# Gated linear attention with experts: scores of two heads beside each other, by halves of the keys

## Chip, core, metric

One Trainium2 chip, of which the kernel uses one core. The time is that of the device for one execution, in microseconds, as the median of several. The engines named below are TensorE (PE; its weight loads are listed apart as PEld), VectorE (DVE), ScalarE (ACT), GpSimd (POOL) and SyncE (SP, which only issues DMAs here).

## What is computed

A linear attention whose state decays by a complex factor at each step, then a top-1 mixture of 8 experts on its rows (B=4, H=8, S=768, D=48; 3072 tokens, 384 features, expert width 1024). Cut to what matters:

```python
for t in range(S):
    ar, ai = a_re_n[:, :, t, :, None], a_im_n[:, :, t, :, None]   # |a| at most 0.999
    S_re, S_im = ar * S_re - ai * S_im + k_t v_t^T, ar * S_im + ai * S_re
    y[:, :, t] = q_t @ S_re
x = y as (B*S, H*D)
e_idx = argmax(x @ w_gate);  gate_w = softmax(...)[e_idx];  eom = sigmoid(x @ w_output_gate)
out[mask] = gate_w * eom * (relu(x[mask] @ w1[e]) @ w2[e])       # mask: e_idx == e
```

Within a tile of 128 time steps the output of query `t` needs the keys `s <= t` of the tile alone and the state before the tile. So a tile costs a matrix of scores (keys by queries, masked to `s <= t`), its product with `v`, and a product of the queries with the state.

## The kernel before

The tokens are cut into 24 tiles of 128 steps (6 tiles for each of 4 batches), and the attention stage goes through them in order; the experts' stage follows it. All matmuls that matter here are f32.

For tile `i` the functions inside `attention` do this:

- `decay`, `turns`, `phase` (a side chain that runs ahead of the tiles): cumulative sums of log-magnitude and phase by matmuls with triangles (L510, L563), a carry of the phase from one tile to the next (L565, or a small DMA of one row, L573), and cosine and sine on ACT into `trig`. The last row of the decay goes through a DMA `rcs` (L519) and a transpose into `rc`.
- `turn`: on DVE, `k` and `q` times cosine and sine (`kc`, `qc`: 128 x 8 heads x 96, L611); on PE eight transposes each into PSUM, on ACT two copies into `kt` and `qt` (96 rows, 8 heads x 128 columns, L621).
- `score` (twice, four heads each): per head one matmul, stationary `kt` of the head (96 rows, 128 columns), moving `qt` (128 columns), into 128 columns of a PSUM bank `sc` (L653); then on DVE one product with a mask into `scores` (L654).
- `state`: the state that the tile leaves, through matmuls with 32 stationary columns (L638), the former state being added by a matmul with the identity (L633).
- `values`: per pair of heads (`j`, `u` = 0 or 1), stationary `v` of the head (48 columns) and moving `scores` (L667), then stationary state and moving `qt` (L673), both into PSUM partitions 0 to 47 for `u` = 0 and 64 to 111 for `u` = 1 of the same tile `xo`; ACT copies it to `xt` (L677).
- `finish` and `gates`: four transposes of `xt`, rows out to `xd` (L700), logits by matmuls with 32 stationary columns (L233).

An f32 matmul stands in the trace as two records, a transpose as one.

PE, DVE and ACT keep an order that is laid out when the kernel is built: the functions are generators, `main` takes the tiles' steps, `step_aside` the side chain's, and the pace and the priorities (`urge`) decide how they are interleaved. Loads are issued on SP's queue in the order of the program; `loads` hands them out as tiles are done: `k`, `q`, `v` have seven buffers each (`AHEAD`), so the load of tile `i + 7` waits for the last reader of tile `i`.

## Time and profile before

| | us |
|---|---|
| median of 3 runs (lowest, highest) | 530.51 (528.88, 531.61) |
| the profiled execution | 532.94 |
| its span, first to last instruction | 531.1 |
| mean granted TensorE clock | 0.975 of full speed |
| PE busy with scores, L653 (384 records) | 51.2 |
| PE busy with values, L667 (384 records) | 41.4 |
| DVE busy with the masked copies, L654 (48) | 32.6 |

The attention stage ends, and the experts' stage begins, at about 283 us. "Busy" is the time in which an engine had at least one instruction in work; PE's records overlap each other, so the busy time of a group is more than its share of the stream. In rows by group, the columns are line, engine, operation, tiles as out<-in, shapes and count, busy us and mean ns of one, and idle time ahead with what ended it. In rows of the timeline they are start, time, engine, line, operation, tiles, shape (stationary rows*columns, then the moving operand), and count.

### The profile page before, as it was taken

What the parts mean: (1) busy time and instruction counts of PE and PEld (TensorE: products, weight loads), DVE (VectorE), ACT (ScalarE), POOL (GpSimd) and SP (SyncE); (2) the same over time, 40 slices, a digit from 0 to 9 for tenths busy, and PEclk for the clock granted to TensorE, in tenths of its full rate; (3) what the DMA queues carried; (4) which work ended last, traced back from release to release, by engine and by line L of the source; (5) the groups of instructions that cost most, each with busy time, mean ns of one, the idle gap of its engine ahead of it and who ended that gap; (6) DMA issues with size and microseconds to landing.
All of it is one profiled execution on the core that took longest, in us unless ns stands there. A gap on an engine that the chain in (4) does not pass through costs nothing.

```text
span 531.1 us, 11170 instructions
## 1 busy us (share of the span) xinstructions
PE 493.5 (93%) x4297; PEld 420.3 (79%) x4297; DVE 337.3 (64%) x775; ACT 319.0 (60%) x603; POOL 121.1 (23%) x131
## 2 busy tenths in 40 slices
PE   2799897998999999999899999999999999999992
PEld 0376565776777778878678889999999999999992
DVE  4578869895998899987685646355453726345220
ACT  7689678985879888767533447355453727354220
POOL 4000201030040503051350554412333222011112
PEclk9799989998999999999999999999999999999997
DMA  8664452534334321014560576525263644330001
GB/s 274 199 231 150 74 165 69 161 77 114 124 76 136 58 90 41 29 31 136 138 207 0 149 191 198 153 101 206 47 209 114 200 123 147 139 135 30 21 22 45
DMA packets 47523, 63.86 MB, mean 120 GB/s; under 512 B 12383, under 2 KB 39290, under 8 KB 47460
## 3 DMA queue, kind: packets, MB, share of 16 engines
q1 hardware_dynamic: 39332, 53.64, 33.8%
q0 software_dynamic: 8128, 9.42, 6.1%
q8 instruction: 36, 0.59, 0.5%
q14 instruction: 27, 0.22, 0.2%
HBM read 53.92 MB, written 9.88 MB: 120 GB/s over the span
## 4 chain that ended last, share of the span: by engine, by line
PE 57%; issue 17%; DMA 7%; DVE 7%; POOL 4%; ACT 4%; SPq 1%; POOLq 0%; DVEq 0%; ACTq 0%
PE up L1225 13%; PE acc L1163 12%; PE tr L95 8%; PE sc L653 4%; PE cs L563 4%; PE xo L667 3%; POOL out_dram L1176 3%; PE cs L510 3%; DMA carry<-ai 2%; PE xo L673 2%; PE st L638 2%; DMA ar<-in_a_re_dram 2%; PE cs L565 1%; POOL rows L1104 1%; PE xt L95 1%
## 5 line engine op out<-in xcount | busy, mean ns | idle before, releaser
L1230 DVE SCALAR_TENSOR_TENSOR hl<-up,hh 128x464 fp32r<-128x464 f32 (+7 forms) x64 | 37.7, 589 | 68.8 <-ACT hh L1229 67.5
L1229 ACT ACTIVATE hh<-up 128x464 fp32r<-128x464 f32 (+7 forms) x64 | 33.1, 518 | 74.0 <-PE up L1225 72.7
L1225 PE MATMUL up<-xh,w1h 128*128 128x464 f32 (+7 forms) x192 | 68.6, 357 | 0.0
L1225 PE MATMUL up<-xl,w1h 128*128 128x464 f32 (+7 forms) x192 | 67.6, 352 | 0.0
L1225 PE MATMUL up<-xh,w1l 128*128 128x464 f32 (+7 forms) x192 | 67.5, 351 | 0.0
L1163 PE MATMUL acc<-hh,w2h 128*128 128x464 f32 (+6 forms) x168 | 61.4, 366 | 0.0
L1176 POOL DMA_INDIRECT out_dram<-y,sid x28 | 31.8, 1135 | 124.5 <-ACT y L1198 121.6
L1163 PE MATMUL acc<-hl,w2h 128*128 128x464 f32 (+6 forms) x168 | 59.4, 356 | 0.0
L1163 PE MATMUL acc<-hh,w2l 128*128 128x464 f32 (+6 forms) x168 | 59.3, 353 | 0.0
L653 PE MATMUL sc<-qt,kt 96*128 96x128 f32 x384 | 51.2, 277 | 0.0
L653 PEld LDWEIGHTS sc<-qt,kt 96*128 96x128 f32 x384 | 47.3, 192 | 2.4 <-issue 1.1
L1104 POOL DMA_INDIRECT rows<-xd,sid x28 | 37.3, 1333 | 51.4 <-DVE w1l L203 22.6
L1059 POOL DMA_INDIRECT table<-entry,addr x20 | 31.4, 1571 | 65.3 <-DVE addr L1055 59.0
L203 DVE TENSOR_TENSOR w1l<-raw,w1h 128x512 fp32r<-128x512 f32 x48 | 30.5, 686 | 20.4 <-ACT w1h L202 17.3
L667 PE MATMUL xo<-scores,v 128*48 128x128 f32 x384 | 41.4, 279 | 0.0
L202 ACT CAST w1h<-raw 128x512 fp32r<-128x512 f32 x48 | 26.9, 619 | 17.0 <-DMA raw<-in_moe_w_dram 17.0
L1225 PEld LDWEIGHTS up<-xl,w1h 128*128 128x128 f32 x192 | 36.0, 188 | 1.2 <-DVE xl L1137 0.3
L1225 PEld LDWEIGHTS up<-xh,w1l 128*128 128x128 f32 x192 | 36.1, 188 | 1.0
L1225 PEld LDWEIGHTS up<-xh,w1h 128*128 128x128 f32 x192 | 36.1, 188 | 0.9
L203 DVE TENSOR_TENSOR w2l<-raw,w2h 128x512 fp32r<-128x512 f32 x48 | 30.5, 686 | 9.8 <-ACT w2h L202 7.4
L533 POOL COPY rcs<-rcs 24x48 f32<-24x48 f32 (+2 forms) x10 | 5.8, 579 | 134.0 <-DMA rcs<-re 86.9
L654 DVE TENSOR_TENSOR scores<-sc,mask 128x512 f32<-128x512 f32 x48 | 32.6, 681 | 5.0 <-PE sc L653 4.5
(214 smaller groups left out, 1125.2 us busy)
## 6 DMA issues: line engine op xcount, KB each, us to landing
raw<-in_moe_w_dram SPq DMA_DIRECT2D x32, 768.0 KB
ar<-in_a_re_dram SPq DMA_DIRECT2D x24, 192.0 KB
ai<-in_a_im_dram SPq DMA_DIRECT2D x24, 192.0 KB
k<-in_k_dram SPq DMA_DIRECT2D x24, 192.0 KB
q<-in_q_dram SPq DMA_DIRECT2D x24, 192.0 KB
v<-in_v_dram SPq DMA_DIRECT2D x24, 192.0 KB
xd<-xn SPq DMA_DIRECT2D x24, 192.0 KB
rows<-xd,sid POOLq DMA_INDIRECT x28
```

The source lines that it names most:

```text
L95: return nc.tensor.transpose(out=out, in_=in_, identity=ident[p0:p0 + n, p0:p0 + n])
L203: ins = nc.vector.tensor_tensor(out=lo[:, s], in0=raw[:, s], in1=hi[:, s].bitcast(F32), op=ALU.subtract)
L653: nc.tensor.matmul(sp[:, j * P:(j + 1) * P], r["kt"][:D2, h, :], r["qt"][:D2, h, :], start=True, stop=True)
L654: nc.vector.tensor_tensor(out=r["s"][:, 4 * hh:4 * hh + 4, :], in0=sp.rearrange("p (h t) -> p h t", t=P), in1=mask.unsqueeze(1).broadcast_ ...
L667: nc.tensor.matmul(op[u * DP:u * DP + D, j * P:(j + 1) * P], vt[c][:, h * D:(h + 1) * D], r["s"][:, h, :], start=True, stop=(cc == 0))
L1059: ins = nc.gpsimd.indirect_dma_start(out=table, out_offset=bass.IndirectOffsetOnAxis(ap=addr[:, c:c + 1], axis=0), in_=entry[:, c, :], in_ ...
L1104: nc.gpsimd.indirect_dma_start(out=rows[e % 2][:n, i, :], out_offset=None, in_=xd[:known], in_offset=bass.IndirectOffsetOnAxis(ap=ids[:n, ...
L1163: nc.tensor.matmul(accs[kt][:, :cap], w[:, cs], a, start=(ft == 0 and s == 0), stop=(ft == FT - 1 and s == 2))
L1176: ins = nc.gpsimd.indirect_dma_start(out=out, out_offset=bass.IndirectOffsetOnAxis(ap=ids(e)[:n, i:i + 1], axis=0), in_=y[:n, :], in_offse ...
L1225: nc.tensor.matmul(up[:, :cap], w[:, kt, :], x[:, kt, :], start=(m == 0), stop=(m == 3 * KT - 1))
L1229: nc.scalar.activation(out=hh, in_=up[:, :cap], func=AF.Relu)
L1230: nc.vector.scalar_tensor_tensor(out=hl, in0=up[:, :cap], scalar=0.0, in1=hh.bitcast(F32), op0=ALU.max, op1=ALU.subtract)
```

## The change

A matrix of scores has keys (rows) by queries (columns), and the block of later keys by earlier queries is zero. The change splits keys and queries into halves of 64. For two heads, the even one and the odd one of a pair, it makes three 64 x 64 blocks each, in four matmuls with 64 stationary columns instead of two with 128: the even head's first keys by all queries go to PSUM partitions 0 to 63, the odd head's first keys by all queries to partitions 64 to 127; the odd head's second keys by second queries to partitions 0 to 63, the even head's to 64 to 127. A pair then fills 3 x 64 columns over 128 partitions in place of 2 x 128, and the masked product reads 384 columns for four heads in place of 512.

In `values`, the first 64 queries of both heads share one block of 64 columns: its stationary operand is `vz`, a copy of `v` with zeros in the 64 rows of the other head. For the second 64 queries the even head's keys stand in order (stationary `v`) and the odd head's with halves exchanged (stationary `vs`). So each head gets two matmuls with 64 moving columns in place of one with 128. `vz` and `vs` are loaded by four more DMAs a tile (64 partitions, 192 elements, 48 KB each) into four buffers each; the zeros are written once by POOL. On the host, `v` is laid out with the even heads ahead of the odd ones; `at_v` is a head's place in it. POOL also makes the new `masks`.

```diff
+    at_v = lambda h: h % 2 * HP + h // 2
+    HALF = P // 2
...
+    masks = const.tile([P, 3, HALF], F32, name="masks")
+    nc.gpsimd.memset(masks, 1.0)
+    for p0, blocks in ((0, (0, 2)), (HALF, (0, 1))):
+        for n in blocks:
+            nc.gpsimd.affine_select(
...
+            VBUFS = 4
...
+            first_v = [pre.tile([P, H, D], F32, name=f"vz{n}") for n in range(VBUFS)]
+            for t in first_v:
+                nc.gpsimd.memset(t[HALF:, 0:HP, :], 0.0)
+                nc.gpsimd.memset(t[:HALF, HP:H, :], 0.0)
+            other_v = [pre.tile([P, HP, D], F32, name=f"vs{n}") for n in range(VBUFS)]
...
+            def loads_halves(i):
+                rows = v.rearrange("b (c x t) h d -> (b c) x t h d", x=2, t=HALF)[i]
+                z, o = first_v[i % VBUFS], other_v[i % VBUFS]
+                nc.sync.dma_start(out=z[:HALF, 0:HP, :], in_=rows[0, :, 0:HP, :])
+                nc.sync.dma_start(out=z[HALF:, HP:H, :], in_=rows[0, :, HP:H, :])
+                nc.sync.dma_start(out=o[:HALF], in_=rows[1, :, HP:H, :])
+                nc.sync.dma_start(out=o[HALF:], in_=rows[0, :, HP:H, :])
...
             def score(i, hh):
...
-                for j in range(4):
-                    h = 4 * hh + j
-                    nc.tensor.matmul(sp[:, j * P:(j + 1) * P], r["kt"][:D2, h, :], r["qt"][:D2, h, :], start=True, stop=True)
+                for j in range(2):
+                    e, o = 4 * hh + 2 * j, 4 * hh + 2 * j + 1
+                    kt, qt = r["kt"][:D2], r["qt"][:D2]
+                    to = sp[:, j * 3 * HALF:(j + 1) * 3 * HALF].rearrange("p (x t) -> p x t", t=HALF)
+                    parts = qt.rearrange("p h (x t) -> p h x t", t=HALF)
+                    nc.tensor.matmul(to[:HALF, 0:2, :], kt[:, e, :HALF], parts[:, e], start=True, stop=True)
+                    nc.tensor.matmul(to[HALF:, 0:3:2, :], kt[:, o, :HALF], parts[:, o], start=True, stop=True)
+                    nc.tensor.matmul(to[:HALF, 2, :], kt[:, o, HALF:], qt[:, o, HALF:], start=True, stop=True)
+                    nc.tensor.matmul(to[HALF:, 1, :], kt[:, e, HALF:], qt[:, e, HALF:], start=True, stop=True)
...
             def values(i):
...
+                vz, vs = first_v[i % VBUFS], other_v[i % VBUFS]
                 for j in range(HP):
+                    by_block = r["s"][:, j, :].rearrange("p (x t) -> p x t", t=HALF)
                     for u in range(2):
-                        h = 2 * j + u
                         nc.tensor.matmul(
-                            op[u * DP:u * DP + D, j * P:(j + 1) * P], vt[c][:, h * D:(h + 1) * D], r["s"][:, h, :],
-                            start=True, stop=(cc == 0))
+                            op[u * DP:u * DP + D, j * P:j * P + HALF], vz[:, at_v(2 * j + u), :], by_block[:, 0, :],
+                            start=True, stop=(cc == 0), skip_group_check=True)
+                    for u in range(2):
+                        nc.tensor.matmul(
+                            op[u * DP:u * DP + D, j * P + HALF:(j + 1) * P], vs[:, j, :] if u else vt[c][:, j * D:(j + 1) * D],
+                            by_block[:, 1 + u, :], start=False, stop=(cc == 0), skip_group_check=True)
...
             def loads():
+                while halves and st["done"] > halves[0] - VBUFS:
+                    loads_halves(halves.pop(0))
...
             loads_b(0, "v")
             loads_b(1, "v")
+            for i in range(2):
+                loads_halves(i)
             loads_b(2)
```

The rows below are the order in which instructions stand on an engine (line, operation, out<-in, shape of what is written, count). On PE, at the scores of tile 0, between the transposes of tile 1's `k` and `q`, before:

```order
L95 MATMUL tr<-ident,kc_162 96x128 x8
L653 MATMUL sc<-qt_165,kt_166 128x128 x4
L95 MATMUL tr<-ident,qc_161 96x128 x8
L653 MATMUL sc<-qt_165,kt_166 128x128 x4
L95 MATMUL cs<-ident,rcs 96x8
```

and after the change, up to the transposes of `q`:

```order
L97 MATMUL tr<-ident,kc_168 96x128 x8
L684 MATMUL sc<-qt_187,kt_188 64x128
L685 MATMUL sc<-qt_187,kt_188 64x2x64
L686 MATMUL sc<-qt_187,kt_188 64x64
L687 MATMUL sc<-qt_187,kt_188 64x64
L684 MATMUL sc<-qt_187,kt_188 64x128
L685 MATMUL sc<-qt_187,kt_188 64x2x64
L686 MATMUL sc<-qt_187,kt_188 64x64
L687 MATMUL sc<-qt_187,kt_188 64x64
L97 MATMUL tr<-ident,qc_167 96x128 x8
```

The place is the same; four matmuls that write 128 partitions have become eight that write 64, between neighbours that write 96. Later in the program the scheduler also puts other work inside a pair, as here, on PE at the scores of tile 2:

```order
L684 MATMUL sc<-qt_187,kt_188 64x128
L97 MATMUL tr<-ident,kc_168 96x128 x4
L97 MATMUL st<-ident,ls 128x128
L97 MATMUL tr<-ident,kc_168 96x128 x4
L685 MATMUL sc<-qt_187,kt_188 64x2x64
```

One matmul of the pair stands ahead of nine transposes, its partner behind them. On SP, the queue around the eighth `carry`, before:

```order
L519 DMA rcs<-re 8x1x48
L700 DMA xd<-xn 128x384
L365 DMA v<-in_v_dram 128x384
L573 DMA carry<-ai 1x16x24
L365 DMA k<-in_k_dram 128x384
```

and after:

```order
L547 DMA rcs<-re 8x1x48
L740 DMA xd<-xn 128x384
L410 DMA vz_173<-in_v_dram 64x192
L411 DMA vz_173<-in_v_dram 64x192
L412 DMA vs_185<-in_v_dram 64x192
L413 DMA vs_185<-in_v_dram 64x192
L601 DMA carry<-ai 1x16x24
L385 DMA v<-in_v_dram 128x384
L385 DMA k<-in_k_dram 128x384
```

The four loads of halves stand ahead of `carry`, and `v` behind it.

More of the change, by code (lines that the diff above doesn't have):

```diff
@@ L112, in tile_gated_attention_moe @@
     nc.gpsimd.tensor_copy(out=tri_o, in_=mask)
+    masks = const.tile([P, 3, HALF], F32, name="masks")
[3 more added lines that the diff above has]
+            nc.gpsimd.affine_select(
+                out=masks[p0:p0 + HALF, n, :], in_=masks[p0:p0 + HALF, n, :], pattern=[[1, HALF]], compare_op=ALU.is_ge,
+                fill=0.0, base=0, channel_multiplier=-1)
     tri_s = tri("tri_s", 1.0, strict=True, dt=BF16)
@@ L445, in prep_exp @@
                     if g == 0:
-                        spare = [wk.tile([P, H, P], F32, name="scores") for _ in range(2)] + [t[1] for t in turned_cats]
+                        spare = [wk.tile([P, HP, 3 * HALF], F32, name="scores") for _ in range(2)] + [t[1] for t in turned_cats]
                         st["spare"] = [t.rearrange("p h t -> p (h t)") for t in spare]
@@ L639, in state @@
                             sp[m:m + MS, h * D:(h + 1) * D], r["k"][:, h, :, :].rearrange("p a b -> p (a b)")[:, m:m + MS],
-                            d["v"][c][:, h * D:(h + 1) * D], start=(cc == 0), stop=True, skip_group_check=True)
+                            d["v"][c][:, at_v(h) * D:(at_v(h) + 1) * D], start=(cc == 0), stop=True, skip_group_check=True)
                 rcb = rc[:, i, :].unsqueeze(2).broadcast_to([D2, H, D])
@@ L648, in score @@
                 if hh == 0:
-                    r["s"] = wk.tile([P, H, P], F32, name="scores")
+                    r["s"] = wk.tile([P, HP, 3 * HALF], F32, name="scores")
                 sp = pp.tile([P, 512], F32, name="sc")
-                for j in range(4):
-                    h = 4 * hh + j
-                    nc.tensor.matmul(sp[:, j * P:(j + 1) * P], r["kt"][:D2, h, :], r["qt"][:D2, h, :], start=True, stop=True)
+                for j in range(2):
[7 more added lines that the diff above has]
+                    nc.tensor.matmul(to[HALF:, 1, :], kt[:, e, HALF:], qt[:, e, HALF:], start=True, stop=True)
                 nc.vector.tensor_tensor(
-                    out=r["s"][:, 4 * hh:4 * hh + 4, :], in0=sp.rearrange("p (h t) -> p h t", t=P),
-                    in1=mask.unsqueeze(1).broadcast_to([P, 4, P]), op=ALU.mult)
+                    out=r["s"][:, 2 * hh:2 * hh + 2, :], in0=sp[:, :6 * HALF].rearrange("p (j t) -> p j t", j=2),
+                    in1=masks.rearrange("p x t -> p (x t)").unsqueeze(1).broadcast_to([P, 2, 3 * HALF]), op=ALU.mult)
                 yield
@@ L674, in values @@
                                 op[u * DP:u * DP + D, j * P:(j + 1) * P], xs[:D2, h * D:(h + 1) * D], r["qt"][:D2, h, :],
-                                start=False, stop=True)
+                                start=False, stop=True, skip_group_check=True)
                 xt = wk.tile([P, HP, P], F32, name="xt")
@@ L884, in attention @@
                 todo += [(loads_a, g)] + [(loads_b, i) for i in range(starts[g], starts[g] + sizes[g])]
+            halves = list(range(2, NT))
             def loads():
+                while halves and st["done"] > halves[0] - VBUFS:
+                    loads_halves(halves.pop(0))
                 while todo and st["early"] >= HOLD.get((todo[0][0] is loads_a, todo[0][1]), 0) and (st["phases"] > todo[0][1] - 3 if todo[0][0] is loads_a else st["done"] > todo[0][1] - AHEAD):
@@ L1303, in recurrence @@
                     for b in range(B):
-                        r = g * R + b * H
-                        nc.sync.dma_start(out=vt[r:r + H], in_=vv[b][:, bass.ds(t0, TB), :])
+                        for h in range(H):
+                            r = g * R + b * H + h
+                            nc.sync.dma_start(out=vt[r:r + 1], in_=vv[b][at_v(h):at_v(h) + 1, bass.ds(t0, TB), :])
                 ar, ai = tiles["ar"], tiles["ai"]
@@ L1446 @@
         a = _np.asarray(inputs[name])
-        a = _np.ascontiguousarray(a if name.startswith("moe") else a.transpose(0, 2, 1, 3))
+        if not name.startswith("moe"):
+            a = a.transpose(0, 2, 1, 3)
+        if name == "v":
+            a = _np.concatenate([a[:, :, 0::2], a[:, :, 1::2]], axis=2)
+        a = _np.ascontiguousarray(a)
         arrays[f"in_{name}_dram"] = a
```

## Prediction

> **What bounds the kernel now.** I read the page first, then the busy time by stage, then single stretches of the TensorE stream.
>
> ```profile
> span 531.1 us, 11170 instructions
> PE 493.5 (93%) x4297; PEld 420.3 (79%) x4297; DVE 337.3 (64%) x775; ACT 319.0 (60%) x603; POOL 121.1 (23%) x131
> PE 57%; issue 17%; DMA 7%; DVE 7%; POOL 4%; ACT 4%; SPq 1%; POOLq 0%; DVEq 0%; ACTq 0%
> 0.00:60.00 60.00, 46.30 (x495) 31.63 (x495) 42.89 (x94) 44.80 (x79) 9.79 (x42) 0.94 0.60 193
> 60.00:140.00 80.00, 70.93 (x736) 50.74 (x735) 63.28 (x150) 63.39 (x113) 6.34 (x6) 0.91 0.46 121
> 140.00:252.00 112.00, 110.16 (x1403) 87.33 (x1392) 98.35 (x263) 88.26 (x167) 25.31 (x18) 1.00 0.27 75
> 252.00:283.00 31.00, 28.20 (x345) 22.71 (x344) 20.35 (x58) 13.80 (x30) 12.34 (x7) 1.00 0.52 148
> by line: issue 41.6%; DMA rows<-xd,sid 17.4%; POOL rows L1104 10.2%; POOL table L1059 5.9%; DVE w1l L203 5.8%; PE sc L998 5.5%; PE sc L1012 4.4%; DMA raw<-in_moe_w_dram 4.2%; PE st L1012 2.9%; PE st L998 2.7%; DVE addr L1055 0.5%; POOLq L11
> ```
>
> The four rows in the middle are stages (start:end, length, then busy us of PE, PE's weight loads, DVE, ACT, POOL, then granted clock). The attention stage, the only one that the change touches, fills 0 to about 283. There PE is busy 70.9 of 80 us and then 110.2 of 112, so a microsecond more or less of TensorE work counts nearly in full from 60 to 252. From 252 to 283 the chain of waits (last row) runs mainly through issue, POOL and DMA, so little of PE's work is on the path there. The 248 us after it belong to the experts.
>
> A busy PE says nothing about how it is spent; that takes the stream itself. An f32 matmul leaves two records, a transpose one.
>
> ```profile
> 132.67 0.60 PE L95 MATMUL tr<-ident,kc 128*96 128x128 f32 x4
> 133.11 1.95 PE L653 MATMUL sc<-qt,kt 96*128 96x128 f32 x16
> 135.06 0.32 PE L95 MATMUL tr<-ident,qc 128*96 128x128 f32 x1
> 129.74 0.39 PE L673 MATMUL xo<-qt,state 96*48 96x128 f32 x4
> ...
> 130.62 0.39 PE L673 MATMUL xo<-qt,state 96*48 96x128 f32 x4
> ```
>
> (Start, time, engine, line, tiles, stationary rows*columns, moving operand, records.) The scores: 16 records in 1.95 us, the last of which takes some 0.275, so (1.95 - 0.275) / 15 = 0.112 us a record. They join the transposes without loss: four transposes at 0.109 end the line at 132.67 + 0.44 = 133.11, where the scores start. The values of two heads, 48 stationary columns each, stand at PSUM partitions 0 and 64: from 129.74 to 130.62 four groups of four records pass, 0.22 us a group, 0.055 a record. So two matmuls in different halves of the columns **run at once**, each record at 0.110, and this is what the change uses for the scores.
>
> **The price of changing column width.** The same view shows what happens where the stationary width changes between over 64 columns (whole array), 33 to 64 (halves) and up to 32 (quarters):
>
> ```profile
> 95.48 0.60 PE L95 MATMUL tr<-ident,xt 128*128 128x128 f32 x4
> 96.01 0.31 PE L667 MATMUL xo<-scores,v 128*48 128x128 f32 x1
> 152.27 0.39 PE L673 MATMUL xo<-qt,state 96*48 96x128 f32 x4
> 152.59 0.53 PE L95 MATMUL tr<-ident,kc 128*96 128x128 f32 x3
> 131.06 0.39 PE L673 MATMUL xo<-qt,state 96*48 96x128 f32 x4
> 131.38 0.91 PE L510 MATMUL cs<-l,tri_l 128*128 128x384 f32 x2
> 136.02 0.81 PE L510 MATMUL cs<-l,tri_l 128*128 128x384 f32 x2
> ```
>
> Four transposes from 95.48 make room at 95.48 + 0.44 = 95.92; the values start at 96.01, **0.09 late**, and their first record takes 0.31 for 0.27: its weights, pulled ahead elsewhere, are now waited for (0.04 for 48 columns, so 0.053 for 64 as an estimate). The other way: the last pair of the group from 152.27 starts at 152.38 and needs 0.11, so 152.49; the transposes start at 152.59, 0.10 late, and three take 0.53 for 0.27 + 2 x 0.109 = 0.49, another 0.04. At 131.38 the same 0.1, and 0.91 for 0.81: a full f32 weight load, 0.10. So a change into halves costs 0.095 + 0.053 = 0.148, one out of them 0.135 (transposes) to 0.20 (f32 at 128 columns); I take **0.148** for either.
>
> The Trainium skill names this in "TensorEngine Tiling (Array Packing)", section "Key Properties": changing the tiling mode drains TensorE. It gives no price; "TensorE: Matmul & The Clock Gate", Part 2, adds that weight loads are pulled ahead of matmuls in flight. By both together a change would cost the 0.095 alone; the rows here show the first load on top of it. This is the second rival below.
>
> **The change, part by part.** *Scores on PE.* 96 pairs of heads (24 tiles x 4) cost four records of 0.112, 0.447 us, or 42.9 in all. Now each half of the columns gets two records over 128 queries (0.110) and two over 64. No row has 64; the nearest are half of 0.110 and the state's matmuls, 48 wide in three column groups:
>
> ```profile
> 138.17 0.53 PE L638 MATMUL st<-v,kc 128*32 128x48 f32 x20
> L638 PE MATMUL st<-v,kc 128*32 128x48 f32 x960 | 21.7, 211 | 0.5 <-issue 0.4
> ```
>
> Twenty records are seven rounds of three; (0.53 - 0.21) / 6 = 0.053 a round with the start included. So a 64-wide round lies between 0.053 and 0.07 (that times 64/48); I take 0.056. A pair: 2 x 0.110 + 2 x 0.056 = 0.332, 31.9 in all, **-11.0**. But in the order of instructions 27 of the 52 runs of scores are cut inside a pair by other work, which leaves one half of the columns idle for about 0.1 each: +2.5. Net -8.5.
>
> *Values.* Two heads: before, two rounds of 128 for values and two for state; now four rounds of 64 in place of the two, 4 x 0.056 against 0.22. The causal quarter is not saved here, since the first 64 queries are multiplied with zero rows of `vz`. 0 (bounds 0 to +5, 96 x 4 x (0.07 - 0.056)).
>
> *Changes of width.* The scores used to be as wide as the transposes and state carries around them. Counted through the order of PE's instructions up to the experts, the width (or the 32-row mode of L565 and the ratios) changes 166 times before and **270** after; into halves from the whole array 14 and 65, back 35 and 84. 104 x 0.148 = **+15.4**.
>
> *DVE.* The masked copy shrinks from 512 to 384 elements.
>
> ```profile
> L654 DVE TENSOR_TENSOR scores<-sc,mask 128x512 f32<-128x512 f32 x48 | 32.6, 681 | 5.0 <-PE sc L653 4.5 <-issue 0.2
> L518 DVE TENSOR_TENSOR q<-q,re 128x384 f32<-128x384 f32 x24 | 13.2, 551 | 1.0 <-ACT re L223 1.0
> by line: DMA carry<-ai 12.2%; PE tr L95 11.9%; PE xo L667 8.7%; PE sc L653 8.2%; PE cs L510 7.5%; PE cs L563 5.8%; PE xo L673 5.7%; PE st L638 4.6%; DVE sq L489 4.2%; DVE l L479 4.2%; DVE scores L654 4.0%; DVE ai L545 3.4%; PE tr L233 2.5%;
> ```
>
> 681 to 551 ns, 48 times: 6.2 us of DVE. In the chain from 140 to 200 (last row) the masked copy holds 4.0% of 60 us, 2.4; a fifth of that is 0.5. I take -0.7 for the whole stage; at the most -6.2.
>
> *Loads.* 96 DMAs of 48 KB more, all on SP's queue.
>
> ```profile
> 7.71 0.33 SPq L365 DMA_DIRECT2D k<-in_k_dram  x1
> 15.48 0.43 SPq L365 DMA_DIRECT2D q<-in_q_dram  x1
> 20.38 0.80 SPq L365 DMA_DIRECT2D ai<-in_a_im_dram  x2
> 37.92 0.56 DVE L518 TENSOR_TENSOR q<-q,re 128x384 f32<-128x384 f32 x1 [0.33 <-ACT re L223]
> L519 POOL DMA_DIRECT2D rcs<-re x2 | 1.3, 658 | 8.0 <-ACT re L223 8.0
> SPq L365 <- PE xo L673: 19.5, 10, 5.3
> L365 SPq DMA_DIRECT2D v<-in_v_dram x24: 327/334/1803, 6.7 to 211.1; - x24
>   DMA carry<-ai: 5.7, 5
> ```
>
> At the start eight go ahead of the load at 7.71 and eight behind the gates' weights; at 0.4 to 0.5 us each the queue is 7 us later, of which its own wait from 15.9 to 20.38 takes 4.5. The `k` and `q` of tile 2, the first of them, are used only from 37.9 on (row). The new memsets on POOL (some 13, about 0.2 to 0.3 us) fit into its 8.0 us of waiting. Later, each tile's halves wait for the values of four tiles before, as `v` waits for those of seven before: both at the same point of time, and SP already stands there (19.5 us in 10 waits). Queued behind are the next `carry`, `rcs`, `xd` and loads. Only `carry` is waited for at once (5.7 us in 5 waits, then the cumulative sum on PE): four issues of 0.33 put up to 1.3 us ahead of it, so 0 to +7 over five waits and the start; I take +1.
>
> *Sum.* PE: -8.5 + 15.4 = +6.9. Of this 98% counts in 140:252, 89% in 60:140, 77% in the first 60 us, little in 252:283; 85% as a mean, **+5.9**. With -0.7 and +1.0: +6.2. The profiled execution took 532.94 us, 1.8 over its span of 531.1; it becomes 539.1. It lies 2.4 above the median of 530.51, so on that scale 536.7; I say **536.5**.
>
> **Rivals.** *The drains hide (faster).* PE is idle 25 us of the first 252 (252 less the three rows' 227.4), where a drain costs nothing, and DVE is busy 98 of 112 us, so its 6.2 us could count. The point is where fewer than half of the added changes cost: with 30% of 15.4, 4.6 - 8.5 - 2 = -6, **524.5**. Against it: the rows above were taken in the middle of the stream, and PE idles under 2 us of 112 where most tiles run. 0.11.
>
> *The change of width costs the drain alone.* 104 x 0.095 = 9.9; -8.5 + 9.9 = +1.4 on PE and +1.5 in all, **532**. 0.16, which includes a sum that cancels otherwise.
>
> *SP's queue becomes the wait.* `carry` behind four issues every tile and the start 3 us late: +7 on top, **543.5**. The chain's 12.2% for `carry` speaks for it, the slack of prefetched loads against it. 0.15.
>
> *The change does not do what it says:* scores of unequal length do not run side by side. A pair then takes 4 x 0.110 + 4 x 0.056 = 0.66, +20 us instead of -11: over **560**. The values' rows speak against it. 0.03.
>
> **How the numbers follow.** The forecast holds 0.55. I leave out the lowest part of the first rival and the last one: 528.5 to 546. Faster by over 0.5% (2.65 us, about what a measurement of this kernel tells from no change) 0.11; within 0.5% 0.17, mostly the drain-only case; slower 0.72: the forecast, SP's queue and the last rival.
>
> **What would show it.** In the new profile scores of 64 columns should run in pairs, a run of 32 records lasting about 1.6 us; the step from transposes to scores and back should be 0.09 to 0.1 late, with a first record 0.04 to 0.06 longer; the masked copy should take about 550 ns; stage 140:252 should grow by 3 to 5 us. Wrong would be: changes of width that fall into waits (PE busy less than now), or a chain that shifts to `carry` and DMA.

## The result

The kernel after the change is **slower**: 548.65 us, the median of four runs (543.48 to 548.84), against 531.06 for the kernel before (528.88 to 532.77); ratio 1.031, with 95% between 1.0238 and 1.0382. The same kernel was measured twice more beside later experiments, at 1.020 (1.0121 to 1.0279) and 1.0271 (1.0218 to 1.0324). The ratios are taken from the fast runs of both kernels side by side, not from the two medians, which are 17.6 us apart; by the ratios the change costs some 11 to 16 us. Predicted were 536.5, with a range up to 546: the direction was right, the size too small.

The page of the kernel after, in the lines that answer to those quoted of before (whole span, engines, the stages as start:end, length, then busy us of PE, PEld, DVE, ACT, POOL, the granted clock, DMA share, GB/s):

```profile
span 546.5 us, 12884 instructions
PE 503.0 (92%) x5065; PEld 416.4 (76%) x5065; DVE 333.9 (61%) x775; ACT 319.4 (58%) x603; POOL 120.2 (22%) x144
60.00:140.00 80.00, 70.60 (x939) 48.24 (x938) 61.28 (x146) 60.13 (x103) 9.24 (x8) 0.91 0.51 141
140.00:252.00 112.00, 106.41 (x1648) 78.29 (x1647) 92.77 (x233) 84.52 (x159) 21.67 (x18) 0.98 0.33 86
252.00:297.00 45.00, 41.19 (x620) 32.23 (x619) 28.38 (x96) 23.01 (x49) 11.31 (x8) 1.00 0.53 146
```

The span is 15.4 longer (546.5 against 531.1), and 14.5 of that lie in the attention stage: the first `up` of the experts (L1271, L1225 before) starts at 297.43 instead of 282.96. The stage from 140 to 252 is the one to look at. Before, PE was busy there 110.16 of 112 us at a clock of 1.00; now it is busy 106.41, at 0.98. If only its work had grown, as forecast, the same 112 us would be as full as before. **Waits and a lower clock have come on top.** PE busy less than before is one of the signs that the forecast named for being wrong.

What the change was to do, it does. First the masked copy among the groups by line and form (busy us, mean ns of one, idle time ahead), then a stretch of PE's timeline in the scores:

```profile
L688 DVE TENSOR_TENSOR scores<-sc,masks 128x384 f32<-128x384 f32 x48 | 26.3, 554 | 10.8 <-PE sc L687 10.7
```

```profile
148.10 0.27 PE L684 MATMUL sc<-qt,kt 96*64 96x128 f32 x1
148.11 0.27 PE L685 MATMUL sc<-qt,kt 96*64 96x128 f32 x1
148.21 0.22 PE L686 MATMUL sc<-qt,kt 96*64 96x64 f32 x1
148.22 0.22 PE L687 MATMUL sc<-qt,kt 96*64 96x64 f32 x1
148.27 0.22 PE L686 MATMUL sc<-qt,kt 96*64 96x64 f32 x1
148.27 0.22 PE L687 MATMUL sc<-qt,kt 96*64 96x64 f32 x1
148.32 0.28 PE L684 MATMUL sc<-qt,kt 96*64 96x128 f32 x1
```

L684 and L685, the two heads of a pair, start 0.01 apart: side by side. In these rows a record with 128 columns moves the stream on by 0.11, one with 64 by 0.05 to 0.06, and the masked copy takes 554 ns: the forecast's prices, all three. Over all runs of scores in this trace the medians are 0.111 and 0.058, the means a little higher, 0.118 and 0.071.

The waits are shown best by one place at 190 us, first SP's queue, then DVE and PE (the bracket is the idle time ahead of an instruction and what ended it):

```profile
186.09 0.52 SPq L410 DMA_DIRECT2D vz<-in_v_dram  x1
186.70 0.55 SPq L411 DMA_DIRECT2D vz<-in_v_dram  x1
187.34 0.55 SPq L412 DMA_DIRECT2D vs<-in_v_dram  x1
187.94 0.59 SPq L413 DMA_DIRECT2D vs<-in_v_dram  x1
188.58 0.58 SPq L385 DMA_DIRECT2D v<-in_v_dram  x1
189.25 0.55 SPq L601 DMA_DIRECT2D carry<-ai  x1
```

```profile
187.40 0.54 DVE L596 TENSOR_TENSOR ai<-cs,rnd 128x384 f32<-128x384 f32 x1
...
193.80 0.55 DVE L573 SCALAR_TENSOR_TENSOR ai<-carry,ai 1x384 f32<-1x384 f32 x1 [2.66 <-DMA carry<-ai]
```

```profile
191.95 0.28 PE L666 MATMUL st<-v,kc 128*32 128x48 f32 x4
194.40 0.91 PE L591 MATMUL cs<-ai,tri_t 128*128 128x384 f32 x2 [2.17 <-DVE ai L573]
```

The row that `carry` copies is ready at 187.94, when L596 ends. Its DMA is issued at 189.25, 1.31 late, because SP is still at the last of four halves then, with a `v` behind it, at 0.6 us each. DVE waits for the row until 193.80, 4.55 us after the issue, and PE for DVE until 194.40. What follows is seen in the windows around that wait:

```profile
192.00:195.60 3.60, 1.43 (x11) 0.89 (x10) 1.67 (x3) 0.69 (x2) 0.00 (x0) 1.00 0.47 103
195.70:199.10 3.40, 3.40 (x71) 3.00 (x72) 2.96 (x6) 2.60 (x5) 0.00 (x0) 0.50 0.38 116
199.20:202.50 3.30, 3.30 (x51) 2.60 (x47) 1.12 (x6) 2.85 (x6) 0.00 (x0) 1.00 0.32 97
```

The granted clock falls to 0.50 for the 3.4 us behind the wait, in which PE does half its work: 1.7 us more. So PE lost 2.17 us at a `carry` that was 1.31 late, and then 1.7. Issued on time, the `carry` could have saved 1.31 of the wait at most. And the second loss is not the rule: in two more profiles of the same kernel (`after_again` and `after_third`, below) PE waited 1.52 and 1.62 us at this place, and the clock stayed at 1.00.

### The profile page after: what moved, and what is told of

The parts are those of the page before. It is cut to its first block, busy times and chain, and to the rows that moved or that the text cites. A ratio compares the mean times of both kernels' runs of the same rounds, so it can differ in the third digit from the quotient of the medians.

```text
span 546.5 us, 12884 instructions
## 1 busy us (share of the span) xinstructions
PE 503.0 (92%) x5065; PEld 416.4 (76%) x5065; DVE 333.9 (61%) x775; ACT 319.4 (58%) x603; POOL 120.2 (22%) x144
## 4 chain that ended last, share of the span: by engine, by line
PE 21%; issue 16%; DMA 5%; POOL 4%; DVE 3%; ACT 1%; POOLq 0%; DVEq 0%; ACTq 0%
PE acc L1209 9%; PE up L1271 9%; DMA raw<-in_moe_w_dram 3%; POOL out_dram L1222 3%; DMA rows<-xd,sid 2%; POOL rows L1150 1%; DVE w2l L215 1%; PE xt L97 1%; PE yp L97 1%; DVE w1l L215 1%; POOL table L1105 0%; PE sc L1044 0%; PE yp L813 0%; DVE hl L1276 0%; DVE hot L1074 0%
## 5 line engine op out<-in xcount | busy, mean ns | idle before, releaser
L1276 DVE SCALAR_TENSOR_TENSOR hl<-up,hh 128x464 fp32r<-128x464 f32 (+7 forms) x64 | 37.7, 589 | 68.2 <-ACT hh L1275 65.7
L1275 ACT ACTIVATE hh<-up 128x464 fp32r<-128x464 f32 (+7 forms) x64 | 33.1, 518 | 73.1 <-PE up L1271 71.7
L1271 PE MATMUL up<-xh,w1h 128*128 128x464 f32 (+7 forms) x192 | 68.6, 357 | 0.0
L1271 PE MATMUL up<-xl,w1h 128*128 128x464 f32 (+7 forms) x192 | 67.6, 352 | 0.0
L1271 PE MATMUL up<-xh,w1l 128*128 128x464 f32 (+7 forms) x192 | 67.5, 352 | 0.0
L1150 POOL DMA_INDIRECT rows<-xd,sid x28 | 34.9, 1246 | 55.2 <-DVE w1l L215 25.8
L561 POOL COPY rcs<-rcs 24x48 f32<-24x48 f32 (+2 forms) x10 | 8.9, 893 | 165.9 <-DMA rcs<-re 124.3
L591 PE MATMUL cs<-ai,tri_t 128*128 128x384 f32 x48 | 26.2, 637 | 13.6 <-ACT ai L235 5.5
L1105 POOL DMA_INDIRECT table<-entry,addr x20 | 26.4, 1319 | 51.5 <-DVE addr L1101 47.1
L1271 PEld LDWEIGHTS up<-xl,w1h 128*128 128x128 f32 x192 | 36.0, 188 | 1.2 <-DVE xl L1183 0.3
L1271 PEld LDWEIGHTS up<-xh,w1l 128*128 128x128 f32 x192 | 36.1, 188 | 1.0
L1271 PEld LDWEIGHTS up<-xh,w1h 128*128 128x128 f32 x192 | 36.1, 188 | 0.9
L713 PE MATMUL xo<-qt,state 96*48 96x128 f32 x320 | 36.4, 279 | 0.3 <-issue 0.3
L685 PE MATMUL sc<-qt,kt 96*64 96x128 f32 x192 | 36.4, 284 | 0.0
L684 PE MATMUL sc<-qt,kt 96*64 96x128 f32 x192 | 36.0, 281 | 0.0
```

The costliest lines, as they stand in the source:

```text
L684: nc.tensor.matmul(to[:HALF, 0:2, :], kt[:, e, :HALF], parts[:, e], start=True, stop=True)
L685: nc.tensor.matmul(to[HALF:, 0:3:2, :], kt[:, o, :HALF], parts[:, o], start=True, stop=True)
L713: nc.tensor.matmul(op[u * DP:u * DP + D, j * P:(j + 1) * P], xs[:D2, h * D:(h + 1) * D], r["qt"][:D2, h, :], start=False, stop=True, skip_ ...
L1105: ins = nc.gpsimd.indirect_dma_start(out=table, out_offset=bass.IndirectOffsetOnAxis(ap=addr[:, c:c + 1], axis=0), in_=entry[:, c, :], in_ ...
L1150: nc.gpsimd.indirect_dma_start(out=rows[e % 2][:n, i, :], out_offset=None, in_=xd[:known], in_offset=bass.IndirectOffsetOnAxis(ap=ids[:n, ...
L1271: nc.tensor.matmul(up[:, :cap], w[:, kt, :], x[:, kt, :], start=(m == 0), stop=(m == 3 * KT - 1))
```

## The experiments

**How they are compared.** Ratios are those of the runs, each against the kernel before on the same chip. Beside them stands a table by stage from each kernel's one profile. Marks are the starts of ACT's copies `xt<-xo` of tiles 0, 8 and 20 and the first `up` of the experts; "clock" is when the first half-speed phase, with which every run begins, ends for good; "carry late" is the time from the end of the `ai` that `carry` copies (L596, L568 before) to the issue of its DMA, summed over 18 carries.

| kernel | ratio (95%) | clock | tile 0 | 0 to 8 | 8 to 20 | 20 to experts | carry late |
|---|---|---|---|---|---|---|---|
| before | 1 | 23.4 | 33.1 | 99.0 | 115.1 | 35.7 | 5.2 |
| before_again | 0.9989 (0.9948 to 1.003) | 19.6 | 32.3 | 95.3 | 114.4 | 38.8 | 2.4 |
| after | 1.031 (1.0238 to 1.0382) | 28.4 | 35.7 | 99.6 | 124.4 | 37.7 | 12.2 |
| after_again | 1.020 (1.0121 to 1.0279) | 24.1 | 33.8 | 99.7 | 121.4 | 38.2 | 10.9 |
| after_third | 1.0271 (1.0218 to 1.0324) | 28.3 | 35.4 | 99.7 | 121.9 | 39.9 | 13.2 |
| e_no_halves | none | 24.3 | 33.7 | 95.2 | 117.1 | 36.5 | 2.2 |
| e_late | 1.0206 (1.0114 to 1.0299) | 25.1 | 34.5 | 98.9 | 120.9 | 39.5 | 11.0 |
| e_cols64 | 1.0262 (1.017 to 1.0353) | 29.2 | 36.7 | 96.2 | 123.3 | 37.3 | 3.9 |
| e_vals64 | 1.0075 (1.0028 to 1.0122) | 28.2 | 35.6 | 100.2 | 114.5 | 38.4 | 2.1 |
| e_halves_pool | 1.0092 (1.0054 to 1.013) | 19.5 | 32.2 | 98.1 | 119.3 | 38.5 | 2.0 |
| e_carry_pool | 1.0326 (1.0266 to 1.0386) | 24.4 | 33.8 | 100.2 | 126.9 | 38.2 | 13.8 |
| e_loads_b | 1.0103 (1.0028 to 1.0178) | 25.4 | 34.8 | 96.8 | 116.8 | 37.5 | 15.3 |
| e_carry_act | 1.0137 (1.0073 to 1.02) | 24.7 | 34.2 | 101.0 | 115.6 | 37.9 | 2.0 |
| e_carry_act_more | 1.013 (1.0069 to 1.0191) | 23.3 | 33.3 | 101.5 | 119.3 | 36.9 | 3.2 |
| e_carry_act_b | 1.012 (1.0034 to 1.0207) | 23.9 | 33.4 | 97.4 | 117.7 | 38.4 | 1.8 |
| e_slack | 1.022 (1.0151 to 1.0289) | 28.5 | 35.8 | 99.2 | 125.6 | 40.2 | 11.0 |
| e_pool_near | 1.0129 (1.0094 to 1.0164) | 23.9 | 34.6 | 93.4 | 127.1 | 39.7 | 2.1 |

The two profiles of before differ by 3.7 us from tile 0 to 8 and by 3.1 from tile 20 on, so a stage of one profile says no more than that. From tile 8 to 20 they agree within 0.7.

One thing must be kept in mind with all of them. The order on PE is laid out when a kernel is built, and an edit can change it elsewhere too. Up to the experts PE leaves 3730 records in the kernel after; between two profiles of the same kernel 3 to 8 of them stand elsewhere. Against the kernel that it was made from it is 5 in `e_late`, 61 in `e_slack`, some 125 in `e_halves_pool` and `e_carry_pool`, 283 in `e_no_halves`, but some 1100 in the two `e_carry_act`; of the 2962 of the kernel before 439 in `e_loads_b` and 880 in `e_carry_act_b`. So the last ones compare more than what their edit names.

### The loads taken away

```diff
-                nc.gpsimd.memset(t[HALF:, 0:HP, :], 0.0)
-                nc.gpsimd.memset(t[:HALF, HP:H, :], 0.0)
+                nc.gpsimd.memset(t, 0.05)
+            for t in other_v:
+                nc.gpsimd.memset(t, 0.05)
...
-            halves = list(range(2, NT))
+            halves = []
...
-            for i in range(2):
-                loads_halves(i)
```

> The kernel after, without any of the 96 loads of halves of v: vz and vs hold a constant, so the output is not the reference's; PE's instructions stay as they are. Theory W (changes of width, together with the order on PE, make nearly all of the +17.6 us): no more than 3 us come back, 545.5 to 549. Theory L (SP's queue makes what the forecast missed, and through the late start the clock as well): 8 to 11 us come back, 537.5 to 541, the load of k for tile 2 is issued at 7.7 us again instead of 12.8, and the stretch with a low granted clock from 66 to 76 shrinks to the 7 us of before.

With other values the part behind the attention becomes a different one (2780 us in all), so there is no ratio; the attention can be compared. It ends, by the first `up`, at 282.4 instead of 297.4, and at 283.0 in the kernel before: **in this profile all of the loss is gone**. Some 2.0 of the 15 us are the earlier clock (tile 0 at 33.7 instead of 35.7). From tile 8 to 20 it takes 117.1 against 121.4 to 124.4, and from tile 0 to 8 95.2 against 99.6. That is theory L, and more than it asked for; theory W, by which at most 3 us come back, is out. What is left of the change from tile 8 to 20 is 2.3 us over the kernel before (114.8, the mean of two).

### The loads at the start, later

```diff
-            for i in range(2):
-                loads_halves(i)
             loads_b(2)
             loads_b(3)
+            for i in range(2):
+                loads_halves(i)
             load_gates()
...
-                while halves and st["done"] > halves[0] - VBUFS:
+                while halves and st["phases"] > 1 and st["done"] > halves[0] - VBUFS:
```

> The kernel after, with the halves of tiles 0 and 1 loaded behind the loads of tiles 2 and 3, and those of tiles 2 and 3 behind the decay's loads that follow; the loads of later tiles stay. Theory L in its early form (the cost is the start, 16 issues of 0.64 us ahead of the decay's and the keys' loads): 3 to 6 us come back, 543 to 545.5, and the first transposed output leaves at 33 us as before the change instead of 35.7. Theory L in its late form (the steady loads) and theory W: less than 1.5 us, 547 to 550.

543.49 us is what the early form of theory L expected, but the ratio, 1.0206, is that of the kernel after in `after_again`: no gain can be shown. Tile 0 leaves at 34.5; but in `after_again`, with all sixteen loads at the start, it leaves at 33.8, and in `e_no_halves`, with none, at 33.7. What it goes by is the column beside it: with the order of the kernels before and after, tile 0 leaves at 32.2 to 32.3 where the clock comes at 19.5, at 33.1 to 34.2 where it comes at 23.3 to 24.7, and at 35.4 to 36.7 where it comes at 28.2 to 29.2. The same transposes show it, after and before:

```profile
25.49 1.94 PE L97 MATMUL tr<-ident,qc 128*96 128x128 f32 x8
```

```profile
24.43 1.08 PE L95 MATMUL tr<-ident,qc 128*96 128x128 f32 x8
```

Eight transposes take 1.94 us at half the clock and 1.08 at the full one. **The late start was the clock, not the loads.** The Trainium skill, "TensorE: Matmul & The Clock Gate", section "What's actually happening", says that the gate watches a free-running window of 3413 ns, so that the cold phase differs from run to run; the trace agrees: the low stretches here last 3.4, 6.8 or 10.2 us.

### The price of the changes of width, alone

```diff
-                    nc.tensor.matmul(sp[:, j * P:(j + 1) * P], r["kt"][:D2, h, :], r["qt"][:D2, h, :], start=True, stop=True)
+                    for m in range(0, P, 64):
+                        nc.tensor.matmul(
+                            sp[m:m + 64, j * P:(j + 1) * P], r["kt"][:D2, h, m:m + 64], r["qt"][:D2, h, :], start=True, stop=True)
```

> The kernel before, where each head's score matmul is cut into two of 64 stationary columns side by side over all 128 queries: the same PE time for the scores, no loads, no change to the values or to DVE. By the order of instructions the width changes 261 times, 95 more than before. Theory W by the forecast's price (0.148 each, 14.1 us, and some 3 for halves that idle at cuts, 85% of it exposed): +12 to +17, 543 to 548. The rival in which the drains hide: +2 to +6, 533 to 537. Drain alone at 0.095: +8 to +10, 539 to 541.

1.0262, that is +14 us (9 to 19; some +12 without the slowest of its four runs), and 8.5 us from tile 8 to 20 over the mean of before, where half of the tiles lie. The forecast's price gave +12 to +17. Drains that hide (+2 to +6) are excluded; the drain alone (+8 to +10) lies at the lower end of the interval. PE stays full, at full clock:

```profile
132.90:256.10 123.20, 121.18 (x1643) 88.10 (x1642) 101.55 (x259) 92.80 (x174) 21.15 (x18) 1.00 0.27 74
```

121.18 of 123.20 us: here it is work that has grown, not waits.

### The values by halves of the queries, alone

```diff
-                    for u in range(2):
-                        h = 2 * j + u
-                        nc.tensor.matmul(
-                            op[u * DP:u * DP + D, j * P:(j + 1) * P], vt[c][:, h * D:(h + 1) * D], r["s"][:, h, :],
-                            start=True, stop=(cc == 0))
+                    for m in (0, 64):
+                        for u in range(2):
+                            h = 2 * j + u
+                            nc.tensor.matmul(
+                                op[u * DP:u * DP + D, j * P + m:j * P + m + 64], vt[c][:, h * D:(h + 1) * D], r["s"][:, h, m:m + 64],
+                                start=(m == 0), stop=(cc == 0), skip_group_check=True)
```

> The kernel before, where the values of each head are two matmuls of 64 queries instead of one of 128, with no loads added and the scores as before. 170 changes of width against 166. Forecast: a round of 64 queries takes 0.056, so no change, 530 to 533. If a round of 64 costs 0.07 as the upper bound has it: +4 to +5, 535 to 536.

1.0075 (1.0028 to 1.0122), +4.0 us: near the upper bound. Counted in the trace from one record to the next of the same half, a round with 64 queries advances the stream by 0.056 in the median but by 0.064 to 0.065 in the mean, since one in ten takes 0.094 or more (`after` alike). But a round with 128 has such a tail too: before, its median is 0.111 and its mean 0.119. Mean against mean, two rounds of 64 cost 0.010 more than one of 128, 192 times: 1.9 us. By stage only 114.5 against 114.8 stand from tile 8 to 20, and the +1 and +1 elsewhere are within the noise of a profile, so the size rests on the runs.

### The loads' queue, and the carry's

On POOL's queue instead of SP's, in `loads_halves`, four times:

```diff
-                nc.sync.dma_start(out=z[:HALF, 0:HP, :], in_=rows[0, :, 0:HP, :])
+                nc.gpsimd.dma_start(out=z[:HALF, 0:HP, :], in_=rows[0, :, 0:HP, :])
```

> The kernel after, with all 96 loads of halves issued on POOL's queue instead of SP's. Theory Q (the halves' issues of about 0.6 us each on SP stand ahead of the carry and the loads of k and q, and that makes what the forecast missed): the carry is issued within 6 us in all of the time when it is ready, against 12.2 us after the change and 5.2 before it, and the ratio to the kernel before falls from 1.031 to 1.010 to 1.018. Theory M (the halves' traffic itself, or the place of the waits, costs the time, whatever the queue): 1.025 to 1.035.

1.0092 (1.0054 to 1.013), below the range that was expected if the queue is the cause; the carry is late by 2.0 us in all. The bytes and the buffers are the same, and 6 to 12 us have gone (1.0092 against 1.020 to 1.031; of the three intervals of the kernel after, the lowest, from 1.0121, just overlaps). By their profiles it is less: from tile 0 to the experts 255.9 us against 259.3 to 261.8, so 3.4 to 5.9. So it is **the place on SP's queue**, not the bytes. The Trainium skill, "DMA: Bandwidth & Descriptors", section "Issuing engines are not separate DMA queues", says that another issuing engine saves only the sequencer's time, "which is usually small relative to the DMA itself". What moves here is the issuing alone, and by the ratios it was half of the loss or more. That it is the `carry`, of all that stands on SP behind the halves, this run doesn't show. DVE's waits for it, in all, are no shorter: 6.0 us, against 5.3, 7.4 and 4.1 in the three profiles of the kernel after.

Only the carry on POOL's queue:

```diff
-                    nc.sync.dma_start(out=st["carry"], in_=fr[127:128, :])
+                    nc.gpsimd.dma_start(out=st["carry"], in_=fr[127:128, :])
```

> The kernel after, with the carry alone moved from SP's queue to POOL's; the halves stay on SP's. If the carry is the only one that suffers behind the halves: the same gain as with the halves on POOL's queue, 1.010 to 1.018. If the first loads of k, q and the decay behind sixteen halves at the start carry half of it: 1.020 to 1.026. If the carry is not what PE waits for: 1.028 to 1.034, and if POOL is late with it, more.

1.0326, as slow as after. But on POOL the carry was late as well, 13.8 us in all against 12.2, since it stands there behind POOL's own instructions (at 123 us behind three that write `table`). So this run didn't take the lateness away, and it can't speak for or against the carry. It fits that the time stayed when the lateness stayed.

### PE in the order in which it is written

Kernel after and kernel before with PE's order fixed from tile 0 on:

```diff
-            FIXED = NT + 9
+            FIXED = 0
```

> The kernel after, with PE's instructions of the attention in the order in which they are written, from the first tile on. That order has 195 changes of width instead of 270 and cuts no run of scores inside a pair; by the forecast's prices PE works 17 us less than after the change. If changes of width and cut runs are what costs time, 1.000 to 1.010. If PE's waits in that order eat it: 1.030 or more.

1.0999 (1.0931 to 1.1066), 586.18 us.

> The kernel before, with PE's instructions of the attention in the order in which they are written: 105 changes of width instead of 166, by the forecast's prices 13 us less PE work. If these count: 0.980 to 0.990. If the waits of that order eat it: 1.000 to 1.030. The difference to the kernel after in its written order, without any reordering: by PE's prices +4 us, with the loads on SP's queue +8 to +13.

1.0895 (1.0831 to 1.0959), 581.12 us. Both are far slower, by PE's waits: from tile 8 to 20 they take 144.7 and 141.6 us, and the clock is low in seven and eight stretches of the attention. Fewer changes of width are worth nothing if PE stands still for them. The order says little about the change.

### The loads alone, and the carry on a queue that is not late

The kernel before, with `v` loaded a second time in four pieces from SP, which the values read:

```diff
+            VBUFS = 4
+            again = [pre.tile([P, H, D], F32, name=f"va{n}") for n in range(VBUFS)]
...
+            def loads_again(i):
+                rows = v.rearrange("b (c x t) h d -> (b c) x t h d", x=2, t=P // 2)[i]
+                for x in range(2):
+                    for y in range(2):
+                        nc.sync.dma_start(
+                            out=again[i % VBUFS][x * (P // 2):(x + 1) * (P // 2), y * HP:(y + 1) * HP, :],
+                            in_=rows[x, :, y * HP:(y + 1) * HP, :])
...
-                            op[u * DP:u * DP + D, j * P:(j + 1) * P], vt[c][:, h * D:(h + 1) * D], r["s"][:, h, :],
+                            op[u * DP:u * DP + D, j * P:(j + 1) * P], again[i % VBUFS][:, h, :], r["s"][:, h, :],
```

> The kernel before with the 96 loads alone: v of each tile is loaded a second time, in four pieces of 48 KB from SP's queue at the places where the change has its halves, into four buffers of its own that the values then read; scores, values and DVE as before, 167 changes of width. The forecast's term: +1, ratio 1.000 to 1.004. Theory Q (four issues of 0.6 us each per tile on SP, waiting for the values, hold up what is behind them): 1.012 to 1.022, with the carry issued 10 us late in all instead of 5.2.

1.0103 (1.0028 to 1.0178), +5.5 us, with the carry late by 15.3 us in all. Below theory Q's range by its median, but above the forecast's: 1.000 to 1.004 hardly reaches into the interval. SP's queue at one of its carries:

```profile
150.65 2.41 SPq L393 DMA_DIRECT2D va<-in_v_dram  x4
153.15 0.55 SPq L583 DMA_DIRECT2D carry<-ai  x1
```

Four issues, 2.41 us together, and the carry right behind them. So the lateness in all is not the price by itself: 15.3 us of it went with 5.5 here, and 12.2 with 11 to 16 in the kernel after.

The kernel after, and the kernel before, with the carry on ACT's queue (the edit of `e_carry_pool`, with `nc.scalar`):

> The kernel after, with the carry alone on ACT's queue (on POOL's it was as late as on SP's, 13.8 us in all, so that run didn't take the lateness away). If the carry's place behind the halves on SP is what PE pays for: late by less than 6 us in all, and 1.012 to 1.020. If the other loads on SP (k, q, the decay's) pay: 1.025 to 1.032.

1.0137 (1.0073 to 1.02); late by 2.0 us in all. From tile 8 to 20 115.6, as before the change.

> The kernel before, with the carry on ACT's queue. There it is late on SP by 5.2 us in all. If PE pays for that: 0.992 to 0.997. If ACT (busy 90 us of 112) is later with it, or it doesn't matter: 0.998 to 1.006.

1.012 (1.0034 to 1.0207): *slower* by some 6 us, though the carry is no longer late there either (1.8). So the move has a price of its own, which these runs don't explain; the other order on PE, with 165 changes of width between tile 0 and the experts instead of 156, may be part of it. In the kernel after it gained all the same, but there too in another order.

> The kernel after once more, as a measure for the three beside it on the same chip: 1.024 to 1.038, and a first transposed output at 33 to 36.5 us, by when the full clock is granted (in the runs so far from 19.5 to 29.2 us, and the first output 32.2 to 36.7 in the same order, whatever was loaded at the start).

1.020 (1.0121 to 1.0279), the first tile at 33.8 with the clock at 24.1. Against `e_carry_act` beside it the intervals overlap, so both were repeated below.

### What was left open

The halves asked for a tile later than their buffers come free, so that their DMAs don't wait at the head of SP's queue:

```diff
-                while halves and st["done"] > halves[0] - VBUFS:
+                while halves and st["done"] > halves[0] - 3:
```

> The kernel after, with each tile's halves asked for one tile later than their buffers come free, so that they don't stand at the head of SP's queue until the values are done; the number of issues is the same. If the wait at the head of the queue is what costs: 1.008 to 1.015, with the carry late by 6 us or less in all. If the issues alone cost (four of 0.6 us each per tile): 1.020 to 1.031 as before, with the carry late by 9 us or more.

1.022 (1.0151 to 1.0289), the carry late by 11.0: as expected if the issues alone cost. But the edit hardly took away what it was to take away. These are the waits of SP ahead of a tile's first half (us in all, times, longest), in the kernel after and then here:

```profile
SPq L410 <- PE xo L713: 17.4, 12, 3.8
```

```profile
SPq L410 <- PE xo L713: 16.4, 8, 3.7
```

**The wait at the head of the queue and the issues are not told apart by this run.** Two of its carries ended in waits of PE of 1.9 and 2.2 us, at 163.9 and 195.4, each with 3.4 us of half clock behind it.

The halves on POOL's queue, and the scores of a tile written right behind the values of the tile before, in the search for a version that beats both kernels:

```diff
-                    if live(i):
-                        yield from score(i, 0)
...
                     yield from (None for _ in range(n))
+                    if live(i + 1):
+                        yield from score(i + 1, 0)
+                        yield from score(i + 1, 1)
```

(`score(i, 1)` goes in the same way.)

> The kernel after with the halves on POOL's queue (1.0092 in its own run), and the scores of a tile written ahead, right behind the values of the tile before: 249 changes of width instead of 271. By the forecast's price of 0.148 for each and the model of PE's work 3.0 us less: 1.002 to 1.007. If the changes cost nothing there: 1.009. If the scores come too early for the transposes that they need, so that PE waits: 1.015 or more.

1.0129: no gain over 1.0092. The fewer changes (234 between tile 0 and the experts instead of 258) come with new waits of PE for the carry, 3.8 us in two, though the carry is late by only 2.1 in all, and with half clock at 249 and 273.

> The kernel before once more, for its stages: 0.995 to 1.005, tiles 8 to 20 in 113 to 117 us, and from the first transposed output to the experts 248 to 252 us.

0.9989 (0.9948 to 1.003), tiles 8 to 20 in 114.4, and 248.6 us from tile 0 to the experts.

> The kernel after with the carry alone on ACT's queue, in five rounds beside the kernel after itself. If the carry's lateness is what PE pays for: 4 us or more below the kernel after, 1.010 to 1.017, and tiles 8 to 20 in 115 to 118 us against 120 to 126. If the first run of it was luck: within 2 us of the kernel after.

1.013 (1.0069 to 1.0191), 7.5 us below `after_third` by the ratios. Its stage of tiles 8 to 20 takes 119.3, above the 115 to 118 that were expected.

> The kernel after, for the comparison: 1.020 to 1.031, tiles 8 to 20 in 120 to 126 us. Where PE waits 2 us or more for the carry, a stretch of 3.4 us at half the clock follows at once; where it waits 1.7 us or less, none.

1.0271 (1.0218 to 1.0324). The intervals of the two no longer overlap, so the kernel with the carry on ACT's queue is faster: by 3.3 us in the first pair, by 7.5 in the second. How much of that is the carry's lateness, and how much the other order on PE, is not shown. PE's longest wait for the carry in `after_third` was 1.62 us, and no half clock followed it, as expected.

The kernel before with 16 transposes of no use in PE's gaps up to 22 us (W0 = 16 instead of 0):

> The kernel before with 16 transposes of no use in PE's idle time up to 22 us. If the first tile's time goes by when the full clock is granted: granted by 20 us, first transposed output at 31 to 32.5 us, 0.993 to 0.998. If the fillers delay the work of the start: 1.000 to 1.005.

0.998 (0.9939 to 1.0022): no difference. In its profile the fillers stood ahead of the phase's cumulative sums, which started at 20 instead of 16 us, and the full clock came at 22.4, not by 20; the first tile left at 36.5. So what an earlier clock is worth wasn't tried by it, and a version faster than the kernel before was not found.

## Why the prediction was right in direction and wrong in size

**The changes of width (+15.4): right.** Counted in the trace from the last record of one width to the second of the next, beyond the lengths of the two records between, up to 0.17 each, they take 36.6 us between tile 0 and the experts in `e_no_halves` and 36.8 in `after`, against 22.0 before: +14.6 to +14.8. The start of the new width alone is late by 0.09 in the median; this part is +11, the rest is the longer first record. `e_cols64`, which has the price without the saving, cost +14 where 12 to 17 were worked out. The rival in which the drain alone counts is out by this count; by the interval of `e_cols64` alone it would lie at its edge.

**Scores (-8.5) and the masked copy: right, as far as can be told.** The pairs run side by side, at the prices put down by the median and somewhat above them by the mean. What can be counted is their sum with the changes of width. From tile 8 to 20, half of the tiles, the stage without PE's idle time takes 112.9 and 113.3 us in the two profiles of before, and 116.0 to 117.3 in `after_again`, `after_third`, `e_halves_pool` and `e_no_halves`. That is +3 to +4, so +6 to +8 for all tiles; the sum put down for PE was +6.9.

**Values (0, bounds 0 to +5): too low by itself.** Alone they cost +4.0 (1.5 to 6.5). The median of a round was as taken; its mean, against the mean of a round of 128, accounts for 1.9. In the kernel after they don't stand out: with the loads out of SP's way the whole change costs +4.9 us (2.9 to 6.9, from 1.0092), where the forecast without its loads makes +5.2. The parts measured alone don't add up to this: +14 less the saving, and +4, is more. That is open.

**The loads (+1): this step failed, by 5 to 11 us.** As put, "four issues of 0.33 put up to 1.3 us ahead of it, so 0 to +7 over five waits and the start; I take +1". Two things were off in it. An issue of 64 partitions took 0.52 to 0.59 in the rows above, not 0.33, and four of them put 2.4 us ahead of what follows; the carry was 12.2 us late in all, against 5.2 before, and six of 18 were over a microsecond late, against two. And the clock had no place in the sum, though a wait that grows to two microseconds can be paid nearly twice through it. The runs have the term at 6 to 12 us: the halves off SP's queue take 1.020 to 1.031 down to 1.0092 (3.4 to 5.9 us by the profiles).

The way from the queue to the time is shown only in part. Between tile 0 and the experts PE is idle for 14.4 and 15.0 us in the two profiles of before, 19.9 to 21.2 in the three of after, 19.0 in `e_halves_pool` and 13.3 in `e_no_halves`. It runs at half clock for 13.7 in both of before, 17.1, 17.1 and 20.5 in the three of after, 13.7 in `e_halves_pool` and 10.2 in `e_no_halves`, and half of such time is lost. By this the two together make 2.9 to 4.3 of the 3.4 to 5.9 us by which `e_halves_pool` is shorter there. But the half clock also comes without the loads (23.9 in `e_vals64`), and the carry's own waits don't follow its lateness. So it is shown that the loads on SP cost this; that they do it through the carry is argued from single places.

The rival "SP's queue becomes the wait" named the queue and gave 543.5; the three medians of the kernel after are 543.92, 547.3 and 548.65. It got 0.15.

**The start: later than put down, and without effect.** The forecast had the sixteen DMAs in their places and SP 7 us later; it was some 9 us later at the decay's loads (23.54 instead of 14.06). The forecast let it pass because SP's own wait would take most of it up and tile 2 needs its loads late. What the runs show is only that none of it reached tile 0 (`e_no_halves` and `after_again`). The 2.6 us by which tile 0 was late in the first profile were the clock, and they are no part of the change's price.

**In the trace of before the loss through the clock could have been read.** There one carry was late by 1.42 us, on SP behind other loads (a row of PE, then the windows of the wait and behind it):

```profile
125.31 1.18 PE L563 MATMUL cs<-ai,tri_t 128*128 128x384 f32 x2 [2.12 <-DVE ai L545]
121.80:125.30 3.50, 1.39 (x20) 0.69 (x18) 0.59 (x2) 1.04 (x2) 0.00 (x0) 1.00 0.74 206
125.80:129.20 3.40, 3.40 (x50) 2.62 (x50) 1.95 (x4) 1.48 (x3) 0.00 (x0) 0.50 0.21 58
```

A wait of 2.12 us, and at once 3.4 us at 0.50. In `before_again` the same carry was late by 0.32, PE waited for it 0.6 us at most, no half clock followed, and tiles 0 to 8 took 95.3 instead of 99.0.

## What to carry to other kernels

Before a change adds DMAs to a queue, list what else is issued there that an engine waits for at once, take the issue time from DMAs of the same shape, and price a late one at its wait and at the clock that the wait may cost. The same loads on POOL's queue were 6 to 12 us cheaper here by the ratios. And a change that makes matmuls narrower pays for each change of width in the stream: some 100 more of them took 15 us here, more than a quarter less of the scores gave back to PE.

## What the hardware showed that was not expected

The clock falls after shorter waits than thought. In the 17 profiles of the table, between 100 and 281 us, PE stood still (from the end of one record to the start of the next) seven times for 1.3 to 1.58 us, and the clock never fell; 19 times for 1.59 to 2.06 us, and in 11 of them a stretch at half clock began within 1.6 us of the wait's end; eleven times for over 2.1 us, and in ten it began within 1.4 us or had begun. The longest of these waits was 3.0 us. The Trainium skill, "TensorE: Matmul & The Clock Gate", section "Why this matters for your kernels", advises against gaps of PE over some 3 us; here 2 are enough.

Of the start it is only shown that tile 0 follows the clock, from 32.2 to 36.7 us, whatever the loads, in the kernels that keep the order of the start; in `e_warm`, with fillers there, it left at 36.5 with the full clock at 22.4. Between two profiles of the same program this alone was up to 1.9 us (35.7 and 33.8 for the kernel after), 0.35% of its time.
